# Which queue loads the first queries and values: SyncE's or GpSimd's

## The chip, the cores and the metric

The kernel runs on one core of one Trainium2 chip. The metric is the device time of one execution in microseconds; lower is better. A profile of one execution goes with it: its span (first to last instruction seen) and every instruction's time on the five engines TensorE (PE), VectorE (DVE), ScalarE (ACT), GpSimd (POOL) and SyncE (SP).

## The reference

Two layers in a row. The first is a gated linear recurrence with batch 4, 8 heads, 768 steps and head size 48. The second is a feed-forward layer that takes the maximum of two products, 3072 tokens of 384 channels, 1024 hidden.

```python
f = 1.0 / (1.0 + np.exp(-f_logit))
for t in range(S):
    state = f[:, :, t, :, None] * state + np.einsum('bhd,bhe->bhde', k[:, :, t], v[:, :, t])
    y[:, :, t] = np.einsum('bhd,bhde->bhe', q[:, :, t], state)
x = y.transpose(0, 2, 1, 3).reshape(B * S, H * D)
out = np.maximum(x @ w1, x @ w2) @ w_out
```

Inputs and output are float32 in HBM.

## The kernel before, in words

The sequence is cut into 12 spans of 256 steps of one batch entry, numbered s = 4 * window + batch; so spans 0, 1, 2 and 3 are the first windows of the four batch entries. A partition holds two neighbouring steps of all 8 heads.

The order of all work is written by hand, as one long string of words, `ORDER`. Each word is one step of one span on one engine: `Lq1s@13` loads (L) the queries (q) of span 1 from SyncE's queue (s) into slot 13; `V0p` is step V of span 0 on POOL (p). The letter a stands for ACT and v for DVE; for steps with @, the number is a slot (loads) or a PSUM bank. Nothing reorders this: each engine runs its words in the order of the string, and waits are put in where data or a buffer asks for them.

The steps that matter here:

- Lf, Lk, Lq, Lv load gates, keys, queries and values of a span, 384 KB each, in 1024 rows of 384 bytes (L115). Wb, Wa and Wo load the halves of w2, w1 and w_out, 768 KB each, in rows of 2 KB and 1.5 KB (L125, L129). Everything lands in one tile, `slots`, of 22 slots; the weights take slots 0 to 11 at the start, the activations of the first spans 12 to 15. A slot is loaded again when its reader is done: the word's place and the release decide when SP issues it.
- E, F, G (ACT): from the gates, the exponential, the logarithm and `one`. e (DVE or POOL): sum of the two steps of a pair. C (PE): running sums. X and Z (ACT): `inv` and `dec`.
- i and j scale keys and queries (L280, L284), K and Q write them into padded tiles `kp` and `qp` (L291, L294), V writes the values into a padded tile `vb` (L104, three copies). t and u transpose kp and qp on PE (L320), U copies them out (L104), A is the product of queries and keys (L337), m masks it (L345), S applies the state (L367), y adds the values (L387), D is the state's increment (L401), n and N update the state.
- H and Y make the token tile xT (L433). d is the hidden layer's product with `wd` = w1 - w2 (L445), r its ReLU, o the output (L460 with `m2`, the product w2 * w_out, and L463 with w_out), b copies it out and O stores it.
- Once, at the start: ws subtracts the weights on DVE (L536), wp permutes their rows on PE (L544), we stores `wd`; wc, wt and wx cast and transpose w2 and wm multiplies it by w_out (L528). w1 and w2 leave their slots when ws has read them, and the gates of spans 2 and 4 are loaded there.

POOL writes constants first: `tri`, `ident` and `perm` (L134 to L220). DVE needs `tri` for its own constants (L146) and zeroes the padded tiles; PE needs `perm` for wp and `ident` for the transposes.

At the start of the order, SP issues f0, k0, q0, v0, half of w2, f1, the other half of w2, both halves of w1, then q1 (into slot 13, after k0 has been read), v1 (into slot 15, after v0 has been read) and k1. All loads are SP's.

Of the kernel before, what the change touches and what calls it, by code (L numbers as in the profile page):

```python
# [17 lines left out]


ORDER = """  # L20
Lf0s@12 Lk0s@13 Lq0s@14 Lv0s@15 E0a Wb0s F0a Lf1s@12 G0a i0v Wb1s e0v C0@0 Wa0s X0a Wa1s Z0a K0v
V0p j0v t0@0 Lq1s@13 D0@2 Lv1s@15 Q0v E1a n0.0v u0@0 n0.1v F1a U0v@0 e1p wc1a A0.0@0 A0.1@2 G1a
m0.0v@0 Lk1s@12 S0@4 wc0a C1@6 z0v@4 ws1v wt1@7 wc2a m0.1v@2 wp1@0 wx1a@7 ws3v y0 Wo0s Z1a ws0v
we1a@0 wp3@2 H0a@4 ws2v wt2@7 Wo1s we3a@2 wp0@0 j1v X1a wp2@2 Y0v@4 Q1p we0a@0 Lf2s@0 wt0@6 wx2a@7
we2v@2 d0.0@0 d0.1@1 i1v V1a K1v d0.2@2 r0.0a@0 Lf4s@13 u1@4 wx0v@6 t1@4 wo1p d0.3@3 U1v@4 wo0p
D1@0 r0.1a@2 n1.0v A1.0@6 Lq2s@8 A1.1@4 S1@2 wo3a wo2v n1.1v Lk2s@10 m1.0v@6 wm0@0 E2a z1v@2
m1.1v@4 Lv2s@11 wm2@1 F2a E4a e2p y1 Lk4s@0 F4a C2@4 H1v@2 wm1@5 Y1v@2 Z2a e4p G2a Lq4s@13 wn0a@0
C4@6 X2a d1.0@2 i2v wn2a@1 j2v wn1a@5 d1.1@3 Lf3s@9 Z4a Q2v d1.2@0 X4a G4a K2v d1.3@1 V2a Lf5s@8
u2@4 t2@4 r1.1a@0 i4v o0.0@6 U2v@4 K4p Lv4s@11 r1.0a@2 j4v A2.0@0 b0.0a@6 Lq3s@10 D2@2 N1.1p
o0.1@4 n2.0v E3a m2.0v@0 Q4p Lv3s@0 F3a n2.1v S2@0 b0.1a@4 A2.1@2 z2v@0 E5a t4@6 N0.1p m2.1v@2  # L30
Lk3s@13 u4@6 N2.1p o1.0@5 F5a U4v@6 V4a Lf6s@8 e5v G5a y2 j3v b1.0a@5 D4@2 A4.0@6 H2a@0 O0s n4.0v
o1.1@5 m4.0v@6 N4.0p Lk5s@11 V3a e3p Lv5s@9 n4.1v G3a Y2v@0 C5@6 b1.1a@5 C3@7 i3p X5a S4@2 Z3a
A4.1@4 Lq5s@0 z4v@2 d2.0@0 Z5a Q3v X3a d2.1@1 E6a K3v d2.2@6 r2.0a@0 m4.1v@4 d2.3@7 Lq6s@13 t3@0
r2.1a@6 u3@0 i5p y4 D3@4 U3a@0 Lk6s@8 H4v@2 K5p o2.0@6 n3.0v Y4v@2 Lf8s@10 F6a n3.1v S3@0 b2.0v@6
A3.0@2 e6p A3.1@4 m3.0v@2 d4.0@6 Lf7s@11 N4.1p d4.1@7 j5v V5p d4.2@2 z3v@0 r4.0a@6 Lk8s@12 m3.1v@4
d4.3@3 G6a Q5v r4.1a@2 D5@6 O1s y3 j6v C6@5 Lv6s@9 H3a@0 o2.1@2 i6v Z6a Y3v@0 Lq8s@0 X6a E8a N3.1v
F8a t5@0 b2.1v@2 Lv7s@10 u5@0 d3.0@4 U5a@0 e8v d3.1@5 n5.0v Q6v d3.2@2 E7a K6v d3.3@3 Lq7s@13 C8@0
N5.0v r3.1a@2 o4.0@1 V6p r3.0v@4 Lf10s@8 F7a n5.1v G8a e7v N5.1p D6@2 Z8a A5.0@4 b4.0v@1 Lf9s@9
X8a t6@6 j8v u6@6 C7@0 U6a@6 n6.0v o3.0@1 m5.0v@4 N6.0p Lk7s@11 V7p n6.1v X7a i8v A5.1@2 b3.0a@1
Lf11s@15 A6.0@4 S5@6 Z7a j7v o3.1@1 K8p z5v@6 m5.1v@2 Lq9s@10 m6.0v@4 y5 Lv8s@12 S6@2 H5a@6 Q8v  # L40
G7a A6.1@4 E9a o4.1@0 i7p z6v@2 m6.1v@4 F9a b3.1a@1 Y5v@6 e9p y6 E10a O3s t8@4 K7p u8@4 H6a@2
Lk9s@8 G9a d5.0@6 U8v@4 Lq10s@9 b4.1a@0 C9@1 O4s d5.1@7 X9a Y6v@2 N6.1p Z9a d5.2@4 O2s r5.0a@6
d5.3@5 Q7v Lk11s@11 d6.0@0 r5.1a@4 Lq11s@0 j9v A8.0@2 Q9p D7@6 V8a m8.0v@2 u7@4 t7@4 Lv9s@13
d6.1@1 U7a@4 n7.0v d6.2@2 N7.0v n7.1v d6.3@3 j10v E11a o5.0@7 r6.0v@0 r6.1a@2 N7.1v Lv11s@15
A7.0@0 b5.0a@7 D8@2 A7.1@3 F11a n8.0v S7@5 m7.0v@0 o6.0@7 Lk10s@10 F10a e11p G10a z7v@5 N8.0p
m7.1v@3 Lv10s@12 e10p C11@0 b6.0a@7 S8@1 i9v A8.1@3 V9p o5.1@7 z8v@1 m8.1v@3 K9v C10@3 y7 Z10a
b5.1v@7 D9@4 H7a@5 j11v y8 O5s Z11a Y7v@5 o6.1@7 X11a Q11p H8a@1 n9.0v Y8v@1 d7.0@4 b6.1a@7 i10p
G11a d7.1@5 O6s i11v d8.0@6 r7.0a@4 Q10v d8.1@7 N9.0v X10a d8.2@0 V10a K10v d8.3@1 r8.0a@6 K11v
d7.2@2 d7.3@3 r8.1v@0 u10@4 r7.1a@2 t9@6 u9@6 t10@4 t11@0 U9a@6 U10v@4 u11@0 o8.0@2 U11v@0 A9.0@3
b8.0a@2 S9@0 m9.0v@3 A9.1@6 D10@2 o7.1@5 z9v@0 m9.1v@6 V11v A11.0@3 y9 n10.0v D11@6 o7.0@2 n11.0v  # L50
m11.0v@3 N11.0p H9v@0 o8.1@3 b7.0v@2 N10.0v b7.1a@5 Y9v@0 O7s A10.0@4 b8.1a@3 S10@6 m10.0v@4
A10.1@0 d9.0@2 z10v@6 d9.1@3 m10.1v@0 d9.2@4 r9.0a@2 d9.3@5 A11.1@0 r9.1a@4 S11@2 y10 z11v@2
m11.1v@0 o9.0@4 H10a@6 Y10v@6 y11 b9.0a@4 d10.0@0 H11v@2 d10.1@1 d10.2@4 r10.0v@0 o9.1@6 Y11v@2
d10.3@5 d11.0@0 r10.1a@4 d11.1@1 b9.1a@6 d11.2@2 O9s d11.3@3 O8s o10.0@4 r11.1v@2 r11.0v@0 o10.1@3
o11.0@0 b10.0a@4 b10.1a@3 O10s P11.0@1 b11.0a@0 O11s P11.1@0 B11.0v@1 R11.0s B11.1a@0 R11.1s
"""


@with_exitstack
def kernel(  # L60
# [51 lines left out]
    def load(nm, s, e, slot):  # L112
        w, b = divmod(s, B)
        src = sources[nm][b, :, w * W:(w + 1) * W, :].rearrange("h (p two) d -> p h (two d)", two=2)
        engines[e].dma_start(out=slots[:, slot, :].rearrange("p (h x) -> p h x", h=H), in_=src)  # L115
        loaded[s][nm] = slots[:, slot, :].rearrange("p (h two d) -> p h two d", h=H, two=2)

    def staged(i, a):
        return slots[:, 4 * i:4 * i + 4, :].rearrange("p s x -> p (s x)").rearrange("p (a x) -> p a x", a=a)
# [3 lines left out]
    def load_columns(dst, w, e, h):  # L123
        cols = slice(h * d_ff // 2, (h + 1) * d_ff // 2)
        engines[e].dma_start(out=dst[:, :, cols], in_=w.rearrange("(k p) m -> p k m", p=C)[:, :, cols])  # L125

    def load_wo(e, h):
        part = slice(h * FG // 2, (h + 1) * FG // 2)
        engines[e].dma_start(out=wo_f[:, part, :],  # L129
                             in_=moe_w_out.rearrange("(j p) m -> p j m", p=C)[:, part, :])  # L130
# [102 lines left out]
    m2 = consts.tile([C, KT, HD], BF16, name="m2")  # L233
# [10 lines left out]
    def step_E(s):  # L244
        gate[s] = work.tile([C, H, 2, D], F32, name="gate", tag="gate", bufs=2)
        nc.scalar.activation(flat(gate[s]), flat(loaded[s]["f"]), AF.Exp, bias=0.0, scale=-1.0)  # L246

    def step_F(s):
        ell[s] = work.tile([C, H, 2, D], F32, name="ell", tag="ell", bufs=2)
        nc.scalar.activation(flat(ell[s]), flat(gate[s]), AF.Ln, bias=1.0, scale=1.0)  # L250

    def step_G(s):
        one[s] = work.tile([C, H, D], F32, name="one", tag="one", bufs=2)
        nc.scalar.activation(one[s], ell[s][:, :, 1, :], AF.Exp, bias=0.0, scale=-1.0)

    def step_e(s, e):
        engines[e].tensor_add(pad("e", s)[:, :, 0:D], ell[s][:, :, 0, :], ell[s][:, :, 1, :])  # L257

    def step_C(s, b):
        ps, t = banks[:, b, :], pad("e", s)  # L260
        nc.tensor.matmul(out=ps[:, 0:HD].rearrange("p (h d) -> p h d", h=H), lhsT=u_inc,  # L261
                         rhs=t[:, :, 0:D], start=True, stop=True)
        for j in range(NP):
            nc.tensor.matmul(out=ps[:, HD + 2 * j:HD + 2 * j + 2],
                             lhsT=t[:, 2 * j:2 * j + 2, :].rearrange("p h e -> p (h e)"),
                             rhs=ones2, start=False, stop=True, skip_group_check=True)
        cum[s] = ps

    def step_X(s):
        inv[s] = work.tile([C, H, D], F32, name="inv", tag="inv", bufs=2)  # L270
        nc.scalar.activation(inv[s].rearrange("p h d -> p (h d)"), cum[s][:, 0:HD], AF.Exp,  # L271
                             bias=0.0, scale=1.0)

    def step_Z(s):
        dec[s] = work.tile([C, HD + 2 * NP], F32, name="dec", tag="dec", bufs=6)
        nc.scalar.activation(dec[s], cum[s][:, 0:HD + 2 * NP], AF.Exp, bias=0.0, scale=-1.0)
# [272 lines left out]
    def store_wd(part, e, b):  # L549
# [3 lines left out]

    steps = {
        "Lf": lambda s, e, b: load("f", s, e, b), "Lk": lambda s, e, b: load("k", s, e, b),
        "Lq": lambda s, e, b: load("q", s, e, b), "Lv": lambda s, e, b: load("v", s, e, b),
        "Wa": lambda i, e, b: load_columns(w1_f, moe_w1, e, i),
        "Wb": lambda i, e, b: load_columns(w2_f, moe_w2, e, i),
        "Wo": lambda h, e, b: load_wo(e, h),
        "E": lambda s, e, b: step_E(s), "F": lambda s, e, b: step_F(s), "G": lambda s, e, b: step_G(s),  # L560
        "e": lambda s, e, b: step_e(s, e), "C": lambda s, e, b: step_C(s, b),
        "X": lambda s, e, b: step_X(s), "Z": lambda s, e, b: step_Z(s),
# [18 lines left out]
        "ws": lambda i, e, b: subtract(i, e), "wp": lambda i, e, b: permuted(i, b),  # L581
        "we": lambda i, e, b: store_wd(i, e, b),
    }
    for word in ORDER.split():
        key, of, e, b = re.fullmatch(r"([A-Za-z]+)([0-9.]+)([avps]?)@?([0-9]*)", word).groups()
        steps[key](*map(int, of.split(".")), e, int(b or 0))


# [28 lines left out]
```

## Time and profile before

| what | us |
|---|---|
| median of 3 runs | 142.43 (142.34 to 143.59) |
| the profiled execution | 142.46 |
| its span | 140.7 |
| PE busy / DVE / ACT / POOL | 121.1 / 110.0 / 87.5 / 47.0 |
| first step E on ACT | 4.52 |
| V0p on POOL | 9.11 to 11.98 |
| first D on PE | 12.04 |
| first weight difference on DVE | 16.76 |

The page divides the span into 40 slices of 3.5 us and gives each engine's busy share in tenths. The chain of waits follows the work back from the last instruction to what released each step. The timelines give start and duration of each instruction; for a load, the duration is that of its issue (SPq is SyncE's queue), and the landing is told apart from it. The granted TensorE clock was 1.0 throughout.

### The profile page before, as it was taken

Reading aid. Unit: us, or ns where it says so; the run is one execution under the profiler, and the core shown is the slowest. Engines: PE = TensorE matmul, PEld = TensorE weight load, DVE = VectorE, ACT = ScalarE, POOL = GpSimd, SP = SyncE. Lnnn points to the kernel's source line nnn. Section 1 sums busy time; section 2 is a strip of 40 time slices with the busy share of each in tenths; the row PEclk is TensorE's granted clock in tenths of the full one; section 3 lists DMA queues with packets and bytes.
Section 4 is the critical chain, followed back from the end, with each engine's and each line's share of the span. In section 5 each row is a group of like instructions: output and inputs, shape, how many; then the busy total and the mean of one; then the engine's idle time right before and its main releaser. Section 6 shows DMA issues by size and latency. Waiting matters only on the chain.

```text
span 140.7 us, 5377 instructions
## 1 busy us (share of the span) xinstructions
PE 121.1 (86%) x2331; PEld 90.0 (64%) x2331; DVE 110.0 (78%) x196; ACT 87.5 (62%) x145; POOL 47.0 (33%) x68
## 2 busy tenths in 40 slices
PE   0033799896999999999899999997999999999990
PEld 0023679654866786868566786675886668678670
DVE  5666799896879997999979898899688895770510
ACT  3624889569988899499774999724884114303120
POOL 7444205405194536800692842529100100000000
PEclk9999999999999999999999999999999999999999
DMA  4999999999999999999999899999400012000754
GB/s 104 272 329 342 388 281 312 340 241 249 272 262 264 266 267 271 221 275 235 240 277 240 204 259 261 257 224 290 112 13 5 5 40 72 7 0 18 211 125 99
DMA packets 56248, 28.66 MB, mean 204 GB/s; under 512 B 50464, under 2 KB 54688, under 8 KB 56224
## 3 DMA queue, kind: packets, MB, share of 16 engines
q1 hardware_dynamic: 56064, 28.22, 79.3%
q8 instruction: 18, 0.29, 0.9%
q10 hardware_dynamic: 160, 0.10, 0.3%
q14 instruction: 6, 0.05, 0.1%
HBM read 23.59 MB, written 4.72 MB: 201 GB/s over the span
## 4 chain that ended last, share of the span: by engine, by line
PE 49%; DMA 13%; DVE 10%; SPq 8%; issue 6%; POOL 6%; ACT 5%; ACTq 0%; DVEq 0%; POOLq 0%
PE banks L463 16%; PE banks L445 11%; DMA slots<-in_v_dram 8%; PE banks L460 7%; SPq L115 6%; DMA slots<-in_q_dram 4%; POOL vb L104 4%; PE banks L337 4%; PE banks L320 3%; DVE wdn L536 2%; PE banks L387 2%; PE banks L367 2%; PE banks L401 2%; SPq L481 2%; DVE at_m L345 2%
## 5 line engine op out<-in xcount | busy, mean ns | idle before, releaser
L463 PE MATMUL banks<-wo,gT 128*128 128x384 bf16 x184 | 33.7, 326 | 0.0
L445 PE MATMUL banks<-xT,wd 128*128 128x256 bf16 x288 | 33.6, 273 | 0.0
L345 DVE TENSOR_TENSOR at_m<-banks,mask 128x1024 bf16<-128x1024 f32 x24 | 29.1, 1217 | 1.8 <-PE banks L337 1.6
L445 PEld LDWEIGHTS <-wd 128*128 128x128 bf16 x288 | 27.3, 98 | 3.8
L452 ACT ACTIVATE gT<-banks 128x1024 bf16<-128x1024 f32 x18 | 18.4, 1032 | 11.6 <-PE banks L445 11.4
L463 PEld LDWEIGHTS <-gT 128*128 128x128 bf16 x184 | 18.0, 98 | 11.9
L104 ACT COPY ob<-banks 128x384 f32<-128x384 f32 (+1 forms) x19 | 8.9, 468 | 20.1 <-PE banks L463 15.2
L433 DVE SCALAR_TENSOR_TENSOR xT<-tail,gaps,banks 128x256 bf16<-128x256 bf16 x36 | 15.1, 474 | 0.1
L460 PE MATMUL banks<-m,xT 128*128 128x384 bf16 x69 | 15.1, 328 | 0.0
L246 ACT ACTIVATE gate<-slots 128x768 f32<-128x768 f32 x12 | 10.2, 848 | 6.9 <-DMA slots<-in_f_logit_dram 6.9
L104 POOL CAST vb<-slots 128x384 bf16<-128x384 f32 (+2 forms) x15 | 8.7, 614 | 14.2 <-DMA slots<-in_v_dram 14.2
L257 POOL TENSOR_TENSOR e<-ell 128x384 bf16<-128x384 f32 x8 | 8.0, 1001 | 13.5 <-ACT ell L250 13.5
L337 PE MATMUL banks<-trs 48*64 48x128 bf16 x384 | 10.5, 227 | 2.2 <-DVE trs L104 1.9
L418 POOL TENSOR_TENSOR state<-tmp_s,dec 128x256 bf16<-128x256 f32 x10 | 6.4, 647 | 17.8 <-DVE tmp_s L413 17.8
L261 PE MATMUL banks<-e,u_inc 128*128 128x384 bf16 x12 | 4.2, 354 | 9.1 <-DVE e L257 7.9
L454 DVE TENSOR_SCALAR gT<-banks 128x1024 bf16<-128x1024 f32 x6 | 7.2, 1219 | 4.3 <-PE banks L445 4.3
L337 PEld LDWEIGHTS <-trs 48*64 48x64 bf16 x384 | 7.5, 110 | 4.8 <-issue 2.2
L250 ACT ACTIVATE ell<-gate 128x768 f32<-128x768 f32 x12 | 10.0, 844 | 0.4
L294 POOL TENSOR_TENSOR qp<-slots,dec 128x768 bf16<-128x768 f32 x4 | 7.3, 1818 | 8.7 <-ACT inv L271 6.7
L104 ACT COPY trs<-banks 128x2048 bf16<-128x2048 bf16 x5 | 9.3, 1863 | 0.9 <-PE banks L320 0.9
L104 DVE COPY trs<-banks 128x2048 bf16<-128x2048 bf16 x7 | 8.4, 1218 | 1.5 <-PE banks L320 1.5
L291 DVE TENSOR_TENSOR kp<-slots,inv 128x768 bf16<-128x768 f32 x8 | 7.5, 954 | 1.4 <-ACT inv L271 1.2
(73 smaller groups left out, 195.2 us busy)
## 6 DMA issues: line engine op xcount, KB each, us to landing
slots<-in_f_logit_dram SPq DMA_DIRECT2D x12, 384.0 KB, 6.5
slots<-in_k_dram SPq DMA_DIRECT2D x12, 384.0 KB, 5.7
slots<-in_q_dram SPq DMA_DIRECT2D x12, 384.0 KB, 6.2
slots<-in_v_dram SPq DMA_DIRECT2D x12, 384.0 KB, 5.9
out_dram<-ob SPq DMA_DIRECT2D x22, 192.0 KB, 3.6
slots<-in_moe_w_dram SPq DMA_DIRECT2D x4, 768.0 KB, 8.4
slots<-in_moe_w_out_dram SPq DMA_DIRECT2D x2, 768.0 KB, 7.4
out_dram<-ob SPq DMA_DIRECT2D x2, 96.0 KB, 2.2
```

What stands on the lines that cost most here:

```text
L104: (nc.scalar.copy if e == "a" else engines[e].tensor_copy)(out, in_)
L115: engines[e].dma_start(out=slots[:, slot, :].rearrange("p (h x) -> p h x", h=H), in_=src)
L246: nc.scalar.activation(flat(gate[s]), flat(loaded[s]["f"]), AF.Exp, bias=0.0, scale=-1.0)
L250: nc.scalar.activation(flat(ell[s]), flat(gate[s]), AF.Ln, bias=1.0, scale=1.0)
L257: engines[e].tensor_add(pad("e", s)[:, :, 0:D], ell[s][:, :, 0, :], ell[s][:, :, 1, :])
L337: nc.tensor.matmul(out=ps[h * HC:(h + 1) * HC, j % 2, par, :], lhsT=t[rows, h, 0, j, par, :], rhs=t[rows, h, 1, j].rearrange("p a t -> p ( ...
L345: nc.vector.tensor_mul(at[s][:, jj].rearrange("p r j a t -> p (r j) (a t)"), banks[:, b:b + 2, :].rearrange("p r (j x) -> p (r j) x", j=2) ...
L433: engines[e].scalar_tensor_tensor(out=x[:, kt], in0=tails[s], scalar=gaps[:, kt:kt + 1], in1=ps[:, :, kt], op0=ALU.mult, op1=ALU.add)
L445: nc.tensor.matmul(out=ps[:, f, :], lhsT=wd[:, kt, ff * C:(ff + 1) * C], rhs=xT[g][:, kt, :], start=(kt == 0), stop=(kt == KT - 1))
L452: nc.scalar.activation(dst, src, AF.Relu)
L460: nc.tensor.matmul(out=ps, lhsT=xT[g][:, kt, cols], rhs=m2[:, kt, :], start=(kt == 0), stop=False)
L463: nc.tensor.matmul(out=ps, lhsT=gT[g][:, ff, cols], rhs=wo[:, ff, :], start=False, stop=(ff == FG - 1))
```

## The change

The queries and values of spans 0 and 1 are loaded by POOL's queue. q0 and v0 are issued before POOL's constants are written: a short second list, `FIRST`, is worked off ahead of the constants, and it also holds SP's f0 and k0. v1 and q1 are the first words of `ORDER`, so POOL issues them after its constants and before V0p. They go into slots 16 and 17, which nothing else uses; before, they went into slots 15 and 13 when these came free. Otherwise all words stand in the same order. The order of the instructions of PE, DVE and ACT is unchanged; POOL gets four DMA issues and SP loses four.

```diff
 ORDER = """
-Lf0s@12 Lk0s@13 Lq0s@14 Lv0s@15 E0a Wb0s F0a Lf1s@12 G0a i0v Wb1s e0v C0@0 Wa0s X0a Wa1s Z0a K0v
-V0p j0v t0@0 Lq1s@13 D0@2 Lv1s@15 Q0v E1a n0.0v u0@0 n0.1v F1a U0v@0 e1p wc1a A0.0@0 A0.1@2 G1a
+Lv1p@16 Lq1p@17 E0a Wb0s F0a Lf1s@12 G0a i0v Wb1s e0v C0@0 Wa0s X0a Wa1s Z0a K0v V0p j0v t0@0 D0@2
+Q0v E1a n0.0v u0@0 n0.1v F1a U0v@0 e1p wc1a A0.0@0 A0.1@2 G1a m0.0v@0 Lk1s@12 S0@4 wc0a C1@6 z0v@4
...
+FIRST = "Lf0s@12 Lk0s@13 Lq0p@14 Lv0p@15"
+
+
+def words(order):
+    for word in order.split():
+        key, of, e, b = re.fullmatch(r"([A-Za-z]+)([0-9.]+)([avps]?)@?([0-9]*)", word).groups()
+        yield key, tuple(map(int, of.split("."))), e, int(b or 0)
...
         loaded[s][nm] = slots[:, slot, :].rearrange("p (h two d) -> p h two d", h=H, two=2)
+
+    for key, of, e, b in words(FIRST):
+        load(key[1], *of, e, b)
...
-    for word in ORDER.split():
-        key, of, e, b = re.fullmatch(r"([A-Za-z]+)([0-9.]+)([avps]?)@?([0-9]*)", word).groups()
-        steps[key](*map(int, of.split(".")), e, int(b or 0))
+    for key, of, e, b in words(ORDER):
+        steps[key](*of, e, b)
```

More of the change, by code (lines that the diff above doesn't have):

```diff
@@ L20 @@
 ORDER = """
-Lf0s@12 Lk0s@13 Lq0s@14 Lv0s@15 E0a Wb0s F0a Lf1s@12 G0a i0v Wb1s e0v C0@0 Wa0s X0a Wa1s Z0a K0v
-V0p j0v t0@0 Lq1s@13 D0@2 Lv1s@15 Q0v E1a n0.0v u0@0 n0.1v F1a U0v@0 e1p wc1a A0.0@0 A0.1@2 G1a
-m0.0v@0 Lk1s@12 S0@4 wc0a C1@6 z0v@4 ws1v wt1@7 wc2a m0.1v@2 wp1@0 wx1a@7 ws3v y0 Wo0s Z1a ws0v
-we1a@0 wp3@2 H0a@4 ws2v wt2@7 Wo1s we3a@2 wp0@0 j1v X1a wp2@2 Y0v@4 Q1p we0a@0 Lf2s@0 wt0@6 wx2a@7
-we2v@2 d0.0@0 d0.1@1 i1v V1a K1v d0.2@2 r0.0a@0 Lf4s@13 u1@4 wx0v@6 t1@4 wo1p d0.3@3 U1v@4 wo0p
@@ L26 @@
[L26 to L55, printed above, removed]
@@ L56 @@
-"""
+Lv1p@16 Lq1p@17 E0a Wb0s F0a Lf1s@12 G0a i0v Wb1s e0v C0@0 Wa0s X0a Wa1s Z0a K0v V0p j0v t0@0 D0@2
+Q0v E1a n0.0v u0@0 n0.1v F1a U0v@0 e1p wc1a A0.0@0 A0.1@2 G1a m0.0v@0 Lk1s@12 S0@4 wc0a C1@6 z0v@4
+ws1v wt1@7 wc2a m0.1v@2 wp1@0 wx1a@7 ws3v y0 Wo0s Z1a ws0v we1a@0 wp3@2 H0a@4 ws2v wt2@7 Wo1s
+we3a@2 wp0@0 j1v X1a wp2@2 Y0v@4 Q1p we0a@0 Lf2s@0 wt0@6 wx2a@7 we2v@2 d0.0@0 d0.1@1 i1v V1a K1v
+d0.2@2 r0.0a@0 Lf4s@13 u1@4 wx0v@6 t1@4 wo1p d0.3@3 U1v@4 wo0p D1@0 r0.1a@2 n1.0v A1.0@6 Lq2s@8
+A1.1@4 S1@2 wo3a wo2v n1.1v Lk2s@10 m1.0v@6 wm0@0 E2a z1v@2 m1.1v@4 Lv2s@11 wm2@1 F2a E4a e2p y1
@@ new lines @@
+Lk4s@0 F4a C2@4 H1v@2 wm1@5 Y1v@2 Z2a e4p G2a Lq4s@13 wn0a@0 C4@6 X2a d1.0@2 i2v wn2a@1 j2v wn1a@5
+d1.1@3 Lf3s@9 Z4a Q2v d1.2@0 X4a G4a K2v d1.3@1 V2a Lf5s@8 u2@4 t2@4 r1.1a@0 i4v o0.0@6 U2v@4 K4p
+Lv4s@11 r1.0a@2 j4v A2.0@0 b0.0a@6 Lq3s@10 D2@2 N1.1p o0.1@4 n2.0v E3a m2.0v@0 Q4p Lv3s@0 F3a
+n2.1v S2@0 b0.1a@4 A2.1@2 z2v@0 E5a t4@6 N0.1p m2.1v@2 Lk3s@13 u4@6 N2.1p o1.0@5 F5a U4v@6 V4a
+Lf6s@8 e5v G5a y2 j3v b1.0a@5 D4@2 A4.0@6 H2a@0 O0s n4.0v o1.1@5 m4.0v@6 N4.0p Lk5s@11 V3a e3p
+Lv5s@9 n4.1v G3a Y2v@0 C5@6 b1.1a@5 C3@7 i3p X5a S4@2 Z3a A4.1@4 Lq5s@0 z4v@2 d2.0@0 Z5a Q3v X3a
@@ new lines @@
+d2.1@1 E6a K3v d2.2@6 r2.0a@0 m4.1v@4 d2.3@7 Lq6s@13 t3@0 r2.1a@6 u3@0 i5p y4 D3@4 U3a@0 Lk6s@8
+H4v@2 K5p o2.0@6 n3.0v Y4v@2 Lf8s@10 F6a n3.1v S3@0 b2.0v@6 A3.0@2 e6p A3.1@4 m3.0v@2 d4.0@6
+Lf7s@11 N4.1p d4.1@7 j5v V5p d4.2@2 z3v@0 r4.0a@6 Lk8s@12 m3.1v@4 d4.3@3 G6a Q5v r4.1a@2 D5@6 O1s
+y3 j6v C6@5 Lv6s@9 H3a@0 o2.1@2 i6v Z6a Y3v@0 Lq8s@0 X6a E8a N3.1v F8a t5@0 b2.1v@2 Lv7s@10 u5@0
+d3.0@4 U5a@0 e8v d3.1@5 n5.0v Q6v d3.2@2 E7a K6v d3.3@3 Lq7s@13 C8@0 N5.0v r3.1a@2 o4.0@1 V6p
+r3.0v@4 Lf10s@8 F7a n5.1v G8a e7v N5.1p D6@2 Z8a A5.0@4 b4.0v@1 Lf9s@9 X8a t6@6 j8v u6@6 C7@0
@@ new lines @@
+U6a@6 n6.0v o3.0@1 m5.0v@4 N6.0p Lk7s@11 V7p n6.1v X7a i8v A5.1@2 b3.0a@1 Lf11s@15 A6.0@4 S5@6 Z7a
+j7v o3.1@1 K8p z5v@6 m5.1v@2 Lq9s@10 m6.0v@4 y5 Lv8s@12 S6@2 H5a@6 Q8v G7a A6.1@4 E9a o4.1@0 i7p
+z6v@2 m6.1v@4 F9a b3.1a@1 Y5v@6 e9p y6 E10a O3s t8@4 K7p u8@4 H6a@2 Lk9s@8 G9a d5.0@6 U8v@4
+Lq10s@9 b4.1a@0 C9@1 O4s d5.1@7 X9a Y6v@2 N6.1p Z9a d5.2@4 O2s r5.0a@6 d5.3@5 Q7v Lk11s@11 d6.0@0
+r5.1a@4 Lq11s@0 j9v A8.0@2 Q9p D7@6 V8a m8.0v@2 u7@4 t7@4 Lv9s@13 d6.1@1 U7a@4 n7.0v d6.2@2 N7.0v
+n7.1v d6.3@3 j10v E11a o5.0@7 r6.0v@0 r6.1a@2 N7.1v Lv11s@15 A7.0@0 b5.0a@7 D8@2 A7.1@3 F11a n8.0v
@@ new lines @@
+S7@5 m7.0v@0 o6.0@7 Lk10s@10 F10a e11p G10a z7v@5 N8.0p m7.1v@3 Lv10s@12 e10p C11@0 b6.0a@7 S8@1
+i9v A8.1@3 V9p o5.1@7 z8v@1 m8.1v@3 K9v C10@3 y7 Z10a b5.1v@7 D9@4 H7a@5 j11v y8 O5s Z11a Y7v@5
+o6.1@7 X11a Q11p H8a@1 n9.0v Y8v@1 d7.0@4 b6.1a@7 i10p G11a d7.1@5 O6s i11v d8.0@6 r7.0a@4 Q10v
+d8.1@7 N9.0v X10a d8.2@0 V10a K10v d8.3@1 r8.0a@6 K11v d7.2@2 d7.3@3 r8.1v@0 u10@4 r7.1a@2 t9@6
+u9@6 t10@4 t11@0 U9a@6 U10v@4 u11@0 o8.0@2 U11v@0 A9.0@3 b8.0a@2 S9@0 m9.0v@3 A9.1@6 D10@2 o7.1@5
+z9v@0 m9.1v@6 V11v A11.0@3 y9 n10.0v D11@6 o7.0@2 n11.0v m11.0v@3 N11.0p H9v@0 o8.1@3 b7.0v@2
@@ new lines @@
+N10.0v b7.1a@5 Y9v@0 O7s A10.0@4 b8.1a@3 S10@6 m10.0v@4 A10.1@0 d9.0@2 z10v@6 d9.1@3 m10.1v@0
+d9.2@4 r9.0a@2 d9.3@5 A11.1@0 r9.1a@4 S11@2 y10 z11v@2 m11.1v@0 o9.0@4 H10a@6 Y10v@6 y11 b9.0a@4
+d10.0@0 H11v@2 d10.1@1 d10.2@4 r10.0v@0 o9.1@6 Y11v@2 d10.3@5 d11.0@0 r10.1a@4 d11.1@1 b9.1a@6
+d11.2@2 O9s d11.3@3 O8s o10.0@4 r11.1v@2 r11.0v@0 o10.1@3 o11.0@0 b10.0a@4 b10.1a@3 O10s P11.0@1
+b11.0a@0 O11s P11.1@0 B11.0v@1 R11.0s B11.1a@0 R11.1s
+"""
+FIRST = "Lf0s@12 Lk0s@13 Lq0p@14 Lv0p@15"
[3 more added lines that the diff above has]
+        yield key, tuple(map(int, of.split("."))), e, int(b or 0)
```

## The prediction

> **What bounds the kernel now.** I read first the slices of the page, then the chain of waits for the first 36 us, then the timelines of SP and DVE there, then the waits.
>
> ```profile
> PE   0033799896999999999899999997999999999990
> DMA  4999999999999999999999899999400012000754
> GB/s 104 272 329 342 388 281 312 340 241 249 272 262 264 266 267 271 221 275 235 240 277 240 204 259 261 257 224 290 112 13 5 5 40 72 7 0 18 211 125 99
> ```
>
> A slice is 3.5 us. TensorE is full from about 16 us to the end; the DMA engines are full from the second slice to 100 us. The rate is 240 to 280 GB/s where only activations (384 B rows) move, and 340 to 390 where weights (1.5 and 2 KB rows) move. So the start is a race for one resource, and what PE loses before it fills is paid at the end, unless a later PE gap takes it up.
>
> ```profile
> 3.05 5.93 DMA slots<-in_v_dram
> 9.11 2.88 POOL vb L104 x3
> 12.04 0.65 PE banks L401 x22
> ...
> 16.77 0.93 DVE wdn L536
> 17.70 1.14 DVE at_m L345
> 18.84 2.42 DVE wdn L536 x3
> ```
>
> Columns: start, us. The values of span 0 land at 8.98, POOL casts them (V0p) until 11.98, and PE's D0 waits for that. From 16.77 the chain runs on DVE's weight differences (ws, L536).
>
> ```profile
> 6.40 3.34 SPq L125 DMA_DIRECT2D slots<-in_moe_w_dram  x3
> 10.02 1.13 SPq L115 DMA_DIRECT2D slots<-in_q_dram  x1
> 12.01 3.14 SPq L115 DMA_DIRECT2D slots<-in_v_dram  x1
> ...
> 16.69 0.15 DVE L377 COPY look<-banks 128x1 f32<-128x1 f32 x1
> 16.76 0.95 DVE L536 TENSOR_TENSOR wdn<-slots 128x768 bf16<-128x768 f32 x1
> ```
>
> The slots view, narrowed to one issue each, gives the landings: the first half of w1 is issued at 7.9 and takes 8.7 us, so lands at 16.6; the second is issued at 8.5 and takes 10.2, so lands at 18.7. DVE starts the first difference at 16.76 and the next at 18.75. The chain names DVE, but each start is within 0.2 us of its weights: DMA and DVE are both late here. Note also that the queries and values of span 1 (L115 at 10.02 and 12.01) are issued *behind* w1 on SP's queue, so they never delay it.
>
> ```profile
> POOL vb L104 <- DMA slots<-in_v_dram: 4.0, 1, 4.0
> PE banks L401 <- POOL vb L104: 1.4, 1, 1.4
> PE banks L261 <- POOL e L257: 1.2, 1, 1.2
> ```
>
> These are waits in the first 30 to 40 us: the most that an earlier V0p can give PE is 1.4 us, and there is a later 1.2 us gap at 32 us (C2 behind e2p behind E2, whose gates land at 30.2).
>
> [...] The full DMA row agrees with one shared resource[...]. [...] SP's first issue here is busy 0.44 us and lands after 3.8. [...]
>
> **The change, part by part.** Each activation load is 384 KB in 1024 rows of 384 B. At the 262 to 269 GB/s of the 5 to 8 us windows it costs the DMA engines 393 KB / 0.266 = 1.48 us. Call X the time POOL spends on issuing one.
>
> *1. q0 and v0 issued by POOL ahead of its constants.* SP loses two issues (1.16 + 1.26 us), so w2 starts at about 1.85 instead of 4.35. f0 and k0 now share with q0 and v0; v0 lands between 8 [...] and 11 us [...], against 8.98. POOL's constants (0.73 to 5.06, 4.3 us) move by 2X. DVE's constants hang on `tri` and move by 2X less their idle time (0.34 + 0.28 us); they then have 0.94 us of cover before i0 at 6.83. Up to X = 0.8 this costs nothing; for X = 1.5, i0, K0 and Q0 move by about 1.5 us, and Q0 ends near 13.3 instead of 11.83. f0 may come 0.8 us late, in parallel with this.
>
> *2. v1 and q1 issued by POOL between its constants and V0p.* POOL reaches V0p at 0.73 + 4X + 4.33 = 5.06 + 4X, or at v0's landing. X isn't in the trace. Lower bound 0.45 us (SP's own issue with nothing in its way). Upper bound 4 us, an estimate: 1024 rows at 3.9 ns, a third of the rate at which the DMA engines eat them. I take 1.5[...]. V0p then starts at 11.1 (9.11 before), and with 1.5 to 2.9 us of casts (the later V casts take 1.5, this one took 2.87 beside DVE) D0 starts at 12.7 to 14.0, against 12.04. DVE goes from D0 to its first weight difference in 16.76 - 12.04 = 4.7 us, so this path asks for it at 17.4 to 18.7. That is +0.6 to +1.9.
>
> *3. The bytes of v1 and q1 move ahead of the weights.* v1 issues at 5.06 + 2X = 8.1, q1 at 9.6, both in a queue of their own, while SP's queue still holds f1, half of w2 and all of w1. [...]two loads x 1.48 = 2.9 us more ahead of w1. It lands at 16.6 + 2.9 = 19.5 and 18.7 + 2.9 = 21.6. DVE's differences move to 19.6 and 21.7: +2.8 and +2.9. This covers part 2 as long as 5.06 + 4X plus casts and 4.7 stays under 19.5, so to X of about 1.75 to 2.05. DVE is in order: the second mask product, j1, Y0 and i1 queue behind the waiting difference, PE's permutations (L544) wait for its result, and the first d0 matmuls for those. All of it was back to back from 16.7 to 25, so it all moves by 2.9.
>
> *4. What gets the 2.9 us back.* The bytes up to k1 are the same, so k1 still lands at 23.9 and f2 at about 30.2. f2's issue (21.85, released by the last difference) slips to about 24.7, inside the 8.4 us of queue it had ahead of it. ACT's E2 waited 1.24 us for f2; after the change it comes at 31.6 instead of 30.34. On PE, m2's products (28.30) start at about 31.2 and end at 34.0, y1 follows to 35.0, so C2 comes at 35.0 instead of 33.18: +1.8, the 1.2 us gap taken up. After this PE is full, its gaps sum to 1.5 us until 97, and SP's order is the old one; I let the 1.8 run to the end.
>
> *5. Slots 16 and 17.* They were unused. Slot 13 is free sooner, so f4's issue no longer waits for Q1 on POOL (23.89, lands 31.7): at most some tenths for E4, hidden behind E2. SP's shorter queue hides nothing else. With the other edits (the word parser) this is nothing.
>
> Sum: 142.46 (profiled execution: span 140.7 and 1.8 around it; median of the runs 142.43) + 2.9 - 1.1 = 144.3, and 0.2 for i0 and f0 slipping: **144.5 us**. Own range 143.4 (PE's later gaps take up another us) to 145.5 (nothing taken up).
>
> **Rivals.**
> *POOL's issue is the bound (X over 2.1).* V0p moves by 4X - 4.05, less up to 1.4 if the casts run undisturbed, less the 1.1 taken up: X = 3 gives +5.4 to 6.8, about 148.5; X = 4 gives 151.9 to 153.3. [...]
> *No matter.* [...] Then w1 slips by some 0.5 us, v0 lands at 11, and PE's 1.2 us gap takes up the rest: 142.9. [...]
> *Faster.* Two queues may drive the engines better than one: if q0, v0, v1, q1 move at the weights' 380 GB/s, each takes 1.03 us, and four save 1.8. D0 comes up to 1.4 earlier, and w1 slips 2.9 - 1.8 = 1.1 only, which the gap at 32 us takes up; all later loads, in a stretch where the DMA row is full, come 1.8 us sooner, so the PE gaps at 68 to 72 and 88 to 96 (1.5 us) shrink: about 141.0. It decides from w1's landing before 17.7 on. For it: DMA share over 1 at only 262 GB/s. [...]
>
> **How the numbers follow.** Forecast 0.45, POOL's issue 0.28, no matter 0.17, faster 0.10. A measurement of this kernel tells about 1% (1.4 us) from no change. Faster takes its own 0.10; same takes the 0.17; slower is 0.45 + 0.28 = 0.73 (the forecast's own low end, 143.4 to 143.9, lies within 1%, but part of "no matter" lies above it, and I let the two cancel). The range runs from 141.6 (most of "faster" left out) to 152 (X = 4 and up left out): under 0.2 in all.
>
> **What would show it.** POOL rows of DMA issue at 0.7 and near 8 us, with X as their length; V0p at 5.06 + 4X. Right: w2's casts and the first difference at 19 to 20 us, idle before it put down to in_moe_w. Wrong towards worse: DVE waits for D0 or U0 and V0p starts after 13.5. Wrong towards better: the difference still at 16.8, or GB/s over 300 in slices with activations only. Wrong altogether: E2 later than 33 us, which would mean that the gap took up nothing.

## The result, and the profile after

| what | before | after |
|---|---|---|
| median (lowest to highest), us | 142.38 (141.21 to 143.59) | 145.64 (145.45 to 146.26) |
| ratio after / before, 95% interval | | 1.026 (1.023 to 1.030) |
| profiled execution, its span | 142.46, 140.7 | 145.47, 143.7 |
| D0 on PE | 12.04 | 13.48 |
| first half of w1 lands, first difference on DVE | 16.6, 16.76 | 19.8, 19.91 |
| second half of w1 lands, next difference | 18.7, 18.75 | 22.8, 22.89 |
| i1 on DVE | 23.97 | 29.12 |
| E2 on ACT | 30.34 | 33.91 |
| C2 on PE | 33.18 | 36.99 |
| first d1 on PE | 35.12 | 38.89 |

The changed kernel is 3.3 us slower by the medians, 3.0 us by the two profiled executions. In this document ratios are taken over the faster of two states that executions fall into, so a ratio can differ a little from the quotient of two medians (1.000 against 1.002 in e2). The slices of its page (3.6 us each) show where:

```profile
PE   0014559999999999999999999997999999999990
DMA  4999999982999999999999889999420003000844
GB/s 106 282 321 309 322 367 346 280 189 65 284 246 271 258 306 252 275 255 240 275 260 234 216 203 313 268 238 243 113 72 5 0 17 97 7 0 8 216 122 97
```

PE is at 9 tenths from the seventh slice, 21.6 us, on; before it was from the sixth, 17.5, with dips to 8 and 6 in the eighth and tenth. There is a new hole in the DMA row (8 and 2 in the ninth and tenth slices, 29 to 36 us): SP issues f2 at 25.61 instead of 21.85, when w1 has left its slot, and the loads behind it are later with it. From 30 to 60 us the list of waits has only one wait on a load, POOL's for a span's keys, 2.3 us, and the same one was there before (2.4 us).

The timeline of POOL, ACT and DVE around the change (start, us; duration, us; in brackets the idle time before and what ended it):

```profile
1.27 1.05 POOL L124 DMA_DIRECT2D slots<-in_q_dram  x1 [0.82 <-POOLq L612]
2.31 0.89 POOL L124 DMA_DIRECT2D slots<-in_v_dram  x1
7.49 0.92 POOL L124 DMA_DIRECT2D slots<-in_v_dram  x1
8.40 0.88 POOL L124 DMA_DIRECT2D slots<-in_q_dram  x1
10.49 2.93 POOL L113 CAST vb<-slots 128x384 bf16<-128x384 f32 x3 [1.21 <-DMA slots<-in_v_dram]
17.87 1.04 ACT L113 CAST w2b<-slots 128x1024 bf16<-128x1024 f32 x1 [3.39 <-DMA slots<-in_moe_w_dram]
19.91 0.96 DVE L548 TENSOR_TENSOR wdn<-slots 128x768 bf16<-128x768 f32 x1 [1.62 <-DMA slots<-in_moe_w_dram]
22.89 2.69 DVE L548 TENSOR_TENSOR wdn<-slots 128x768 bf16<-128x768 f32 x3 [0.88 <-DMA slots<-in_moe_w_dram]
28.24 0.96 DVE L113 CAST wd<-banks 128x768 bf16<-128x768 f32 x1 [1.02 <-ACT wd L113]
33.91 0.84 ACT L258 ACTIVATE gate<-slots 128x768 f32<-128x768 f32 x1
```

An issue costs POOL 0.9 to 1.05 us. V0p would have been ready to start at 9.28 but waits 1.21 us for v0, and it is 1.4 us later than before. The weights are the larger delay: the second half of w2 (ACT, L113) and both halves of w1 (DVE, L548) end a wait each. The last of POOL's four issues is over at 9.28, before v0 has landed, so POOL's issuing is not what V0p waits for in the end. E2 on ACT follows its predecessor with no wait on a load at all. Before, it had waited for its gates:

```profile
30.34 0.84 ACT L246 ACTIVATE gate<-slots 128x768 f32<-128x768 f32 x1 [1.24 <-DMA slots<-in_f_logit_dram]
```

The chain of waits, 0 to 36 us, agrees: one load carries it from 8 to 23 us.

```profile
8.11 14.68 DMA slots<-in_moe_w_dram
22.89 0.97 DVE wdn L548
23.90 1.65 PE banks L556 x7
25.55 0.85 PE banks L524 x8
26.40 0.99 PE banks L556 x7
...
28.24 0.96 DVE wd L113
```

After it come the difference (DVE), the permutations (PE, L556, with a transpose of w2 between them) and the store of `wd`; i1 stands behind that in DVE's order.

### The profile page after: what moved, and what is told of

It reads as the page before. It is cut to its first block, busy times and chain, and to the rows that moved or that the text cites. A ratio compares the mean times of both kernels' runs of the same rounds, so it can differ in the third digit from the quotient of the medians.

```text
span 143.7 us, 5376 instructions
## 1 busy us (share of the span) xinstructions
PE 122.8 (85%) x2331; PEld 91.1 (63%) x2331; DVE 110.7 (77%) x196; ACT 87.4 (61%) x145; POOL 51.2 (36%) x72
## 3 DMA queue, kind: packets, MB, share of 16 engines
q0 software_dynamic: 448, 1.57, 3.8%
## 4 chain that ended last, share of the span: by engine, by line
PE 71%; DMA 13%; DVE 8%; SPq 2%; ACT 1%; issue 1%; POOL 1%; ACTq 0%; DVEq 0%
PE banks L457 21%; PE banks L475 19%; DMA slots<-in_moe_w_dram 10%; PE banks L472 8%; PE banks L349 4%; PE banks L332 4%; PE banks L399 4%; PE banks L540 3%; DMA slots<-in_f_logit_dram 3%; PE banks L379 2%; PE banks L413 2%; PE banks L556 2%; DVE at_m L357 2%; SPq L137 2%; DVE kp L303 1%
## 5 line engine op out<-in xcount | busy, mean ns | idle before, releaser
L113 ACT COPY ob<-banks 128x384 f32<-128x384 f32 (+1 forms) x19 | 8.9, 467 | 19.9 <-PE banks L475 15.1
L113 POOL CAST vb<-slots 128x384 bf16<-128x384 f32 (+2 forms) x15 | 9.0, 635 | 9.5 <-DMA slots<-in_v_dram 9.5
L306 POOL TENSOR_TENSOR qp<-slots,dec 128x768 bf16<-128x768 f32 x4 | 7.3, 1813 | 12.6 <-DVE slots L296 10.6
L113 ACT COPY trs<-banks 128x2048 bf16<-128x2048 bf16 x5 | 9.3, 1863 | 0.3 <-PE banks L332 0.3
L113 DVE COPY trs<-banks 128x2048 bf16<-128x2048 bf16 x7 | 8.5, 1219 | 1.1 <-PE banks L332 1.0
L303 POOL TENSOR_TENSOR kp<-slots,inv 128x768 bf16<-128x768 f32 x4 | 7.5, 1864 | 4.0 <-DVE slots L292 3.9
```

What stands on the lines that cost most here:

```text
L113: (nc.scalar.copy if e == "a" else engines[e].tensor_copy)(out, in_)
L303: engines[e].tensor_mul(pad("kp", s)[:, :, :, 0:D], by_parity(loaded[s]["k"]), both(inv[s]))
```

## The experiments

Three theories could explain a loss of 3 us. A: the bytes of v1 and q1 now move ahead of w1 (and of the second half of w2, which stands before w1 in SP's queue). B: POOL's time for the issues delays i0, V0p and D0. C: POOL's queue, whatever is in it, disturbs SP's loads. Each kernel is compared with the kernel before on the same chip.

**1. SP alone, with v1 and q1 ahead of w1 (e1).** An edit of the kernel before; no load is POOL's.

```diff
-Lf0s@12 Lk0s@13 Lq0s@14 Lv0s@15 E0a Wb0s F0a Lf1s@12 G0a i0v Wb1s ...
-V0p j0v t0@0 Lq1s@13 D0@2 Lv1s@15 Q0v ...
+Lf0s@12 Lk0s@13 Lq0s@14 Lv0s@15 E0a Wb0s F0a Lf1s@12 Lv1s@16 Lq1s@17 G0a i0v Wb1s ...
+V0p j0v t0@0 D0@2 Q0v ...
```

> SyncE loads everything, as in the kernel before; v1 and q1 are moved ahead of the second half of w2 and of w1 in its queue, into slots 16 and 17. POOL issues nothing. Theory A (the loss is the order of the bytes: 2 x 393 KB ahead of w1): w2's second half is cast near 17.6, the first weight difference at 19.6, the next at 21.7 or somewhat later, +2.0 to +3.2 us on the time of before. Theory B (POOL's issue delays the constants, i0, V0p and D0): nothing of that is left, so 0 +- 0.5 us. Theory C (it is POOL's queue as such[...]): 0 to +0.5 us.

Measured: 145.95 against 141.88 us, ratio 1.028 (1.025 to 1.031). The full loss, with nothing on POOL's queue. DVE's timeline:

```profile
20.73 0.96 DVE L536 TENSOR_TENSOR wdn<-slots 128x768 bf16<-128x768 f32 x1 [4.05 <-DMA slots<-in_moe_w_dram]
22.92 2.70 DVE L536 TENSOR_TENSOR wdn<-slots 128x768 bf16<-128x768 f32 x3
```

D0 is where it was before (11.88), and the second difference is where it is in the changed kernel (22.92 against 22.89). B and C are not needed for the loss. Its size, 4.1 us, is above A's +2.0 to +3.2.

**2. POOL's first pair alone (e2).** q0 and v0 by POOL as in the change; v1 and q1 by SP, at their old places.

```diff
-Lv1p@16 Lq1p@17 E0a Wb0s ... V0p j0v t0@0 D0@2
-Q0v ...
+E0a Wb0s ... V0p j0v t0@0 Lq1s@17 D0@2
+Lv1s@16 Q0v ...
```

> Only q0 and v0 are issued by POOL, before its constants; q1 and v1 are SyncE's again, at their old places behind w1 (into slots 17 and 16). A: D0 still slips by some 1.4 us, but w1 lands at 16.6 and 18.7 as before, so the first weight difference starts at 18.2 (D0's path) and the next at 20: +0.3 to +1.2 us. B: the whole of POOL's delay on D0 is there, so nearly the whole loss, +2.0 to +3.2. C: about half the loss, +1 to +2.

Measured: 142.22 against 141.88 us, ratio 1.000 (0.996 to 1.004). The timeline of POOL and DVE:

```profile
10.17 2.14 POOL L113 CAST vb<-slots 128x384 bf16<-128x384 f32 x3 [2.60 <-DMA slots<-in_v_dram]
17.17 0.95 DVE L548 TENSOR_TENSOR wdn<-slots 128x768 bf16<-128x768 f32 x1
```

The constants are later (i0 at 8.29 instead of 6.83), V0p starts 1.1 us later, the first difference 0.4 us later; C2 is at about 32.7 against 33.18. So POOL's issue delay is real at the head and gone by 33 us: the loss is at or below the low end of A's +0.3 to +1.2, and B, which asked for +2.0 to +3.2, falls. But D0 slips by only 0.3 us here, to 12.36, where 1.4 was expected, so this run tests the late constants and not the whole lateness that D0 has in the changed kernel. That the loss comes without it is shown by e1 and e3.

**3. POOL's second pair alone (e3).** q0 and v0 back on SP; v1 and q1 by POOL. POOL then issues them at 5.03 and 6.08.

```diff
-FIRST = "Lf0s@12 Lk0s@13 Lq0p@14 Lv0p@15"
+FIRST = "Lf0s@12 Lk0s@13 Lq0s@14 Lv0s@15"
```

> Only v1 and q1 are issued by POOL, between its constants and V0p; q0 and v0 are SyncE's. POOL's constants, i0 and K0 keep their times (POOL ready at about 7, v0 at 9 to 10). A: v1 and q1 are ahead of w1 as in the changed kernel: first difference at 19.5 to 20, the next near 22, +2 to +3 us. B: D0 slips by under 1 us, so 0 to +1. C: half, +1 to +2.

Measured: 145.59 us, ratio 1.027 (1.022 to 1.032): the full loss again, 3.7 us and so above A's +2 to +3, with D0 as before (12.06). v1 has landed by 12.6 and q1 by 14.3, both ahead of SP's f1 (15.5), which SP had queued behind half of w2:

```profile
15.54 0.84 ACT L258 ACTIVATE gate<-slots 128x768 f32<-128x768 f32 x1 [6.14 <-DMA slots<-in_f_logit_dram]
20.91 0.96 DVE L548 TENSOR_TENSOR wdn<-slots 128x768 bf16<-128x768 f32 x1 [4.05 <-DMA slots<-in_moe_w_dram]
```

A queue of its own let two loads pass that the kernel before first used at 21.36 (j1) and 23.69 us (V1), and what stood in SP's queue paid.

**4. The whole change, with v1 and q1 late (e4).** Both stay on POOL, but behind e1p, issued at 15.86 and 16.78.

```diff
-Lv1p@16 Lq1p@17 E0a ...
-... U0v@0 e1p wc1a ...
+E0a ...
+... U0v@0 e1p Lq1p@17 Lv1p@16 wc1a ...
```

> As the changed kernel, but v1 and q1 are issued by POOL after e1, at about 15.5 us, when most of w1 has landed. A: the first difference at 18.2 (D0's path), the second half of w1 at 20 to 21[...]: +0.5 to +1.8 us. B: as the changed kernel less V0p's wait, +1.5 to +2.5. C: as the changed kernel, +2.5 to +3.3.

Measured: 144.13 us, ratio 1.015 (1.011 to 1.018). DVE's timeline:

```profile
18.22 0.95 DVE L548 TENSOR_TENSOR wdn<-slots 128x768 bf16<-128x768 f32 x1
20.22 2.69 DVE L548 TENSOR_TENSOR wdn<-slots 128x768 bf16<-128x768 f32 x3
24.66 0.56 DVE L296 SCALAR_TENSOR_TENSOR slots<-gate,slots 128x384 f32<-128x384 f32 x1 [1.76 <-ACT wd L113]
```

No difference waits for w1 any more: that loss is gone. But j1 (L296) waits 1.76 us. The row names ACT, which was long done; q1, issued at 15.86, landed 8.7 us later, at 24.6. Too early delays the weights, too late delays the queries themselves. The 2.25 us lie above A's +0.5 to +1.8 and inside B's +1.5 to +2.5, so the time alone would speak for B; the wait that the trace shows is q1's, which no theory had in its forecast.

**5 and 6. The dose (e5, e6).** In the kernel before, on SP alone: one load (v1) ahead of the second half of w2 and of w1, and three (v1, q1, k1).

```diff
-... Lf1s@12 G0a ...
+... Lf1s@12 Lv1s@16 G0a ...                      (e5; Lv1s@15 taken out)
+... Lf1s@12 Lv1s@16 Lq1s@17 Lk1s@18 G0a ...      (e6; Lv1s@15, Lq1s@13, Lk1s@12 taken out)
```

> All loads from SyncE, and one load (v1, slot 16) ahead of the second half of w2 and of w1, instead of two. If each load ahead costs w1 its 1.45 us on the DMA engines, and the 16 KB instruction packet seen near 18 to 20 us costs another 1.2 us whichever load is in flight then: w2's second half is cast at 16.1, first difference at 18.1 (or 19.3 if the packet meets it), next at 20.2 to 21.4; behind it the PE gap of 1.2 us at 32 us takes up the first part: +0.3 to +1.5 us on the time of before. Rival (a fixed price for breaking the order w2, w1, whatever the number of loads): +3 to +4 as with two.

> All loads from SyncE, and three loads (v1, q1, k1 in slots 16 to 18) ahead of the second half of w2 and of w1. By bytes: one more load than with two, which cost 4.0 us: first difference near 22.1, next near 24.2, +5.0 to +5.8 us on the time of before. Rival of the fixed price: +3.5 to +4.3, as with two.

Measured: 144.25 and 147.83 us against 142.2, ratios 1.015 (1.013 to 1.017) and 1.041 (1.035 to 1.046). With e1 the dose is 0, 1.5, 2.8 and 4.1% for none, one, two and three loads. DVE's first difference in e5, then in e6:

```profile
18.00 0.96 DVE L536 TENSOR_TENSOR wdn<-slots 128x768 bf16<-128x768 f32 x1 [1.26 <-DMA slots<-in_moe_w_dram]
21.38 2.70 DVE L536 TENSOR_TENSOR wdn<-slots 128x768 bf16<-128x768 f32 x3 [1.28 <-DMA slots<-in_moe_w_dram]
```

```profile
22.34 0.96 DVE L536 TENSOR_TENSOR wdn<-slots 128x768 bf16<-128x768 f32 x1 [5.60 <-DMA slots<-in_moe_w_dram]
24.45 2.69 DVE L536 TENSOR_TENSOR wdn<-slots 128x768 bf16<-128x768 f32 x3
```

The time follows w1's landing, and a fixed price for breaking the order, whatever the number of loads, falls: it asked for +3 to +4 us in e5 and +3.5 to +4.3 in e6, and they lose 2.05 and 5.6. But e5 loses more than its +0.3 to +1.5. In it one load of 1.48 us moved the second half by 2.6 us (21.38 against 18.75). Something else is in front of it; see the ledger below. In e1, e5 and e6 the second half of w2 is late too, and no run makes it late by itself. It lands ahead of w1 each time, and each weight difference needs both.

**7 and 8. V0 on ACT (e7, e8).** If D0's path were a limit, V0 on ACT, which is free then, would show it. e7 is e2 with the edit, e8 the kernel before with it.

```diff
-V0p
+V0a
```

> q0 and v0 by POOL ahead of its constants, q1 and v1 by SyncE behind w1 (the version that ran as fast as before), and in addition the copies of V0 on ACT instead of POOL. ACT is idle from 10.8 to 12.4; the copies take 1.05 to 1.2 us there against 2.1 to 2.9 on POOL. If D0's path still counts: D0 about 0.5 us earlier and -0.3 to -0.8 us. If the weights, k1 and f2 bound the start: within 0.3 us of before.

> The kernel before, with only the copies of V0 moved from POOL to ACT, which is idle from 9.4 to 12.5. D0 starts near 10.7 instead of 12.04. If D0's path bounds the start: -0.8 to -1.3 us. If the weights' landing (16.6 and 18.7), k1's (23.9) and f2's (30.2) bound it: 0 to -0.4 us.

Measured: e7 142.16 us, ratio 0.999 (0.997 to 1.001): nothing. e8 143.32 us, ratio 1.008 (1.005 to 1.011): slower, although D0 starts at 10.60 instead of 12.04. DVE in e8:

```profile
17.02 0.96 DVE L536 TENSOR_TENSOR wdn<-slots 128x768 bf16<-128x768 f32 x1 [1.46 <-DMA slots<-in_moe_w_dram]
19.84 2.70 DVE L536 TENSOR_TENSOR wdn<-slots 128x768 bf16<-128x768 f32 x3 [0.72 <-DMA slots<-in_moe_w_dram]
```

An earlier head only waits longer for w1, and the second half of w1 comes 1.1 us *later* than before. With no load moved and w1's first half nearly in place, i1 then starts at 26.17 instead of 23.97. That e8 came out slower was in neither forecast. Both results say that the start is bound by loads and not by D0's path; the second repeats the puzzle of e5. No kernel here beats the one before; e2 and e7 tie with it.

**The ledger of w1.** The narrow views of the DMA queues show, in the first 25 us, one packet that isn't the kernel's data: queue q8, kind "instruction", 16 KB (on the page 18 of them make 0.29 MB). Before, it starts at 18.9 us; after, at 20.1; in e8, at 17.4 (packets, MB, share of 16 engines, for all packets that start in that microsecond):

```profile
q1 hardware_dynamic: 735, 0.28, 122.6%
q8 instruction: 1, 0.02, 7.8%
```

```profile
q8 instruction: 1, 0.02, 7.0%
```

```profile
q8 instruction: 1, 0.02, 7.0%
```

Its 7.0 to 7.8% of 16 engine-microseconds is 1.1 to 1.25 us, the time that this one packet took. If it kept *one* of the 16 engines busy and a load needed all 16, that load would end that much later. This step is the author's estimate: the view shows neither the engine nor how a load is spread over them, and the times of packets overlap (q1's add up to 122.6% in that microsecond). What the landings show is this. Before, the packet started 0.2 us after the second half of w1 had landed (18.7), and q1, for which nobody waits, landed 2.5 us after that half, where such a load takes 1.5. Taking 16.6 and 18.7 from before, 1.5 us for each load ahead and 1.1 us if the packet comes before the half has landed:

| kernel | loads ahead | packet, us | first half: sum, difference starts | second half: sum, next starts |
|---|---|---|---|---|
| before | 0 | 18 to 19 | 16.6, 16.76 | 18.7, 18.75 |
| e8 | 0 | 17 to 18 | 16.6, 17.02 | 19.8, 19.84 |
| e5 | 1 | 18 to 19 | 18.1, 18.00 | 21.3, 21.38 |
| after | 2 | 20 to 21 | 19.6, 19.91 | 22.8, 22.89 |
| e1 | 2 | 18 to 19 | 20.7, 20.73 | 22.8, 22.92 |
| e3 | 2 | 18 to 19 | 20.7, 20.91 | 22.8, 22.91 |
| e6 | 3 | 18 to 19 | 22.2, 22.34 | 24.3, 24.45 |

All agree within 0.4 us, most within 0.2; the 1.5 comes from the kernel before, the 1.1 from the packet's length. Three more kernels have no load ahead of w1: e2 (differences start at 17.17 and 19.17, packet at 19.3), e7 (17.08 and 19.16, packet at 19.0) and e4 (18.22 and 20.22, packet at 20.6). In none of them does the trace show a difference waiting for w1. (In e1, e3 and e6 DVE is busy up to the second start, so there the landing is only known to be no later.) By this reading the packet costs nothing when the load that comes late isn't the one waited for, as before, where it was q1. The expectation of e5 had the packet in it, with 21.4 for the second difference if the packet met that half, and 21.38 was measured. But the packet was never moved by itself, and what fixes its moment isn't known, so this is a reading that these kernels agree with, not a separate test.

## Why the prediction was right, and which terms were off

The direction, the cause and the place were right: step 3, bytes ahead of w1, and not POOL's work, set the time. E1 gives the loss without POOL, and e2 gives POOL's issues ahead of the constants without loss. The size was short: 144.5 predicted and 145.64 measured, just above the prediction's own narrow range of 143.4 to 145.5. That it wasn't further off is in part luck, since two errors of opposite sign partly cancel.

- **Step 1 (constants late, D0 late): right.** i0 moved by 1.45 us against the 1.5 forecast, D0 by 1.44, to 13.48, inside 12.7 to 14.0. f0 wasn't late at all (E0 at 4.46 against 4.52), and the 0.2 us that the sum adds for i0 and f0 has no working behind it.
- **Step 2 (X = 1.5, the author's estimate): too high.** The issues took 1.05, 0.89, 0.92 and 0.88 us. V0p, forecast at 11.1, started at 10.49, and its last wait was for v0's bytes. The choice was harmless because this path was covered either way, as step 3 said it would be; e1 and e3, in which D0 is not late, lose as much as the whole change.
- **Step 3 (w1 at 19.5 and 21.6): right for the first half, short for the second.** 19.8 and 22.8 were measured. The term that was mis-sized is the second one, +2.9 that measured +4.1. Two loads account for 3.0; by the ledger, which is argued in part, the remaining 1.1 is the instruction packet, which came just after this half had landed before, and comes before its landing now. The working moved the landing by bytes alone; the packet's row was there to be read in the profile of before, though not how it would count. That both loads are served ahead of w1 was an assumption of this step, and it is measured: v1 and q1 landed at 15.3 and 17.4. From 13 to 16 us, when they moved beside the second half of w2, POOL's queue and SP's started 48 and 46, 62 and 62, 49 and 48 packets in the three microseconds; POOL's carried 0.59 MB and SP's 0.32.
- **"It all moves by 2.9": short by another 1.0.** i1 moved by 5.15, because DVE waited 1.02 us for ACT's part of `wd` (28.24 in the timeline above), which stands behind PE's permutations in the chain. Before, DVE went from its token step to that store (23.00) without a gap. What had grown is PE's part. The same seven matmuls of a permutation, before and after:

```profile
19.80 0.94 PE L544 MATMUL banks<-wdn,perm 128*128 128x256 bf16 x7
23.90 1.65 PE L556 MATMUL banks<-wdn,perm 128*128 128x256 bf16 x7 [0.33 <-DVE wdn L548]
```

  From here to the first product with `wd` (23.00 and 28.42) PE took 3.2 us before and 4.5 after, with the same instructions. Before, it had run without a gap since 14.86; after, it had just waited 0.92 and 0.33 us for the two differences. In e8, where it waits 0.86 and 0.16 us, the seven take 1.65 us too; in e7 and e6, where PE has no wait right before them but one 2.6 us earlier, 1.45 and 1.40 us. The granted clock reads 1.00 in these stretches before, after, in e8 and in e7, so the reason is not shown. The prediction shifted a stretch that was back to back on DVE as a block of fixed length; a late load made it start later and also run longer.
- **Step 4 (k1 and f2 as before): right on the loads, wrong on who waits.** k1 landed at 24.2 (23.9), f2 at 29.9 (30.2). But E2 came at 33.91, not 31.6. It had no wait on f2: ACT's order, itself behind the late `wd` and d0, was later than the load. E2's 1.24 us of slack was used up, and E2 came 2.3 us later than forecast.
- **"1.1 us taken up": more was.** From i1's +5.15 to C2's +3.8 the old PE gap of 1.22 us and a little more went; from there to the end another 0.8 went, out of PE's later gaps (1.5 us before, between 68 and 96 us; 0.8 after, between 96 and 100). About 2.1 us in all, so the two errors partly cancel: 2.9 - 1.1 + 0.2 = 2.0 forecast, 5.15 - 2.1 = 3.0 measured. The sign that the prediction set for "the gap took up nothing", E2 later than 33, came true without that meaning: E2 was late and the gap was still taken up.
- **Step 5 (slots nothing): nothing in any run speaks against it.** The two slots were not tried by themselves; e2 uses them and loses nothing.
- **The rivals.** *POOL's issue is the bound* needed X over 2.1; it is 0.9 to 1.05. *No matter* needed w1 to slip by only some 0.5 us; it slipped by 3.2 and 4.1. In e3 POOL's two loads were done by 14.3, before SP's f1 (15.5). *Faster* needed w1 before 17.7 and two queues at 380 GB/s. The bytes up to k1 are the same in both kernels, and k1 landed at 24.2 after and 23.9 before: no gain. E1 and e3 agree with one shared resource: the same two loads cost the same from either queue, 1.028 (1.025 to 1.031) and 1.027 (1.022 to 1.032).

## What to carry to other kernels

In this kernel the DMA engines are full at the start (share 1.14 before and 1.08 after, from 3.5 to 18 us), and there the order of bytes is the schedule: the second queue brought no bandwidth (309 GB/s in that stretch, 333 before), it only let its loads pass those of the first (in e3 by 12.6 and 14.3, ahead of f1 at 15.5), and by the ledger each load that passed cost the one waited for its own time (1.5 us per 384 KB). So list the loads by when they are needed before giving one a queue of its own, and move it neither ahead of the weights nor (e4) behind its own deadline. After working out a landing, look also for instruction packets in the narrow DMA windows: here a landing that had come 0.2 us before one lost about a microsecond more when it slipped behind it, and the packet is the argued cause. And where an engine will have to wait for a late load, don't count on its next instructions taking as long as before: here PE's seven matmuls took 1.65 us instead of 0.94.

## What the hardware showed that was not expected

- One 16 KB instruction packet, starting between 17 and 21 us, takes 1.1 to 1.25 us. In the seven kernels of the ledger's table one load, in flight at its start or the next, lands 1.0 to 1.2 us later than the 1.5 us for each load ahead account for. That the packet is the cause is argued.
- The same seven matmuls take 0.94 us after 4.9 us of PE without a gap and 1.65 us behind waits of 0.92 and 0.33 us, at a granted clock of 1.00 in both. No run varies this by itself.
- POOL's issue of a load of 1024 rows of 384 bytes takes 0.88 to 1.05 us, about twice the 0.37 to 0.57 us that an SP issue takes where it is shortest. The two issued while DVE was at work (7.49 to 9.28) took no longer than the two issued while it stood idle (1.27 to 3.2). Its packets are larger than SP's for the same shape:

```profile
q1 hardware_dynamic: 51904, 26.65, 73.1%
q0 software_dynamic: 448, 1.57, 3.8%
```

  That is 3.5 KB a packet on POOL's queue (1.57 MB / 448), where SP's loads of the same rows move in packets of about 384 bytes (SP's queue has 4,160 packets and 1.57 MB fewer than before). It bought no time here: e1 and e3 cost the same.
